# Retention and mixture-of-depths on one core: a new order for the routed work, and constant products on TensorE

## Chip, cores and metric

The kernel runs on 1 core of one Trainium2 chip. The metric is the device time of one execution in microseconds (us); lower is better.

## The reference

Inputs q, k, v have shape (4 batches, 8 heads, 768 tokens, 64). Step one is retention, a recurrence with a decay per head; step two picks 128 of the 768 tokens of each batch by a score and sends only those through a feed-forward block (512 to 1024 to 512).

```python
state = gamma[None, :, None, None] * state + np.einsum('bhd,bhe->bhde', k[:, :, t], v[:, :, t])
y[:, :, t] = scale * np.einsum('bhd,bhde->bhe', q[:, :, t], state)
...
x = np.ascontiguousarray(attn_out.transpose(0, 2, 1, 3)).reshape(B, S, H * D)
...
scores = np.einsum('bsd,d->bs', x, w_gate)
...
top_idx = np.argpartition(-scores[b], capacity)[:capacity]
h = np.maximum(xe @ w1, 0.0)
ye = h @ w2
g = 1.0 / (1.0 + np.exp(-scores[b, top_idx]))
out[b, top_idx] = x[b, top_idx] + g[:, None] * ye
```

## The kernel before

The 4 x 768 tokens are walked in 12 blocks of 256 tokens, three blocks to a batch; block m belongs to batch m // 3, and each block has two chunks of 128 tokens (u = 0, 1). The schedule is written out by hand: one turn of the main loop (L538) for each block, and every engine takes its instructions in the order in which the program issues them.

**A turn m, in program order.** SyncE (SP) issues the load of block m+4 (L540; for the last blocks at L561). POOL scales and casts block m+2 to bf16 (`cast`, L180: qb, kc, vb). TensorE (PE) transposes q of block m+1 (`transposes`, L192), multiplies the second half of the heads' scores (`scores(m, 1)`, L212, whose result VectorE (DVE) multiplies by the mask into am, L224), updates the state (`update`, L251), transposes k of block m+1, forms the output of block m (`inside`, L230, and `across`, L242). ScalarE (ACT) copies the output to xo and DVE multiplies it by w_gate and sums it into the token's score (`finish`, L267). SP writes xo to HBM (`put`, L289). PE then does `scores(m+1, 0)` and `turn_back(m+1)` (L202).

**The routed work** of a batch is cut into functions, and `at(t, place, f, ...)` (L479) hangs each on a place in a turn; `slot_work(t, place)` (L526) issues what hangs there. Places -1, 0, 1, 2, 3 to 5 stand in turn m ahead of the cast, after `update(m, 0)`, after the k transposes, after `put`, and at the turn's end. Within one place the functions come in the order in which L482 to L524 register them. After the last turn, what is left is issued in sorted order (L570), as turns 12 and 13. For the batch that ends in block m the steps are: rows, spread and beats (compare scores), ranks and pick (turn m+1, place 4), split, index and gate (turns m+1 and m+2), `route_fetch` (L414, POOL gathers the 128 rows from HBM by an indirect DMA), `route_turn` (L423, PE transposes them), `ffn_up` in two parts (L438), `ffn_down` (L454), `ffn_add` (L464, DVE), `route_put` (L470, POOL scatters the rows to HBM by an indirect DMA). Batches 0 and 1 fetch at place -1 of turns 6 and 9 and put at place 5 of turns 8 and 11. Batch 2 fetches in turn 10 and puts in turn 13, batch 3 does all of it in turns 12 and 13.

An indirect DMA names a range of HBM rows (`flat[:(b + 1) * S]`), so the fetch of batch b waits until earlier writes to these rows have landed, those of the puts of earlier batches too, and POOL's queue waits with it.

**PSUM.** Eight banks: pt (the transposes, one bank), pa (scores, two), py0 and py1 (outputs, one each), pst (state, one) and two slots of the tag pm, shared by pb, pr, rk, pi, pg, ph and pd. For batches 2 and 3 both parts of `ffn_up` write one two-bank tile in pa's place (L445), and batch 2's `ffn_down` writes in pt's place (L457). `inside` takes py0 and py1 itself (L232).

The lines to follow are

```python
    p, b, m = B - 2, B - 1, NBLK
    at(m - 1, 4, ffn_up, p, 0)
    at(m, 0, ffn_up, p, 1)
    at(m, 1, ffn_down, p)
    at(m + 1, 0, route_index, b)
    at(m + 1, 0, ffn_add, p)
    at(m + 1, 0, route_turn, b)
```

Of the kernel before, what the change touches and what calls it, by code (L numbers as in the profile page):

```python
# [9 lines left out]
FT = mybir.dt.float32  # L10
BF = mybir.dt.bfloat16
# [7 lines left out]
def kernel(ctx: ExitStack, tc: tile.TileContext, q, k, v, w_gate, w1, w2, capacity, out):  # L19
    nc = tc.nc  # L20
    B, H, S, D = q.shape
    C = 128
    NC = S // C
    T = 2 * C
    NM = S // T
# [49 lines left out]
    wgB = consts.tile([128, Dm], FT)  # L75
    nc.sync.dma_start(wgB, bass.AP(tensor=w_gate.tensor, offset=w_gate.offset, ap=[[0, 128], [1, Dm]]))

    part_i = consts.tile([128, 3], I32)  # L80
# [47 lines left out]
        nc.gpsimd.affine_select(out=causal[rows], in_=causal[rows], pattern=[[-1, 2], [1, C]],  # L128
                                compare_op=OP.is_ge, fill=0.0, base=0, channel_multiplier=-2)

    ones = consts.tile([128, 128], BF)
    nc.vector.memset(ones, 1.0)

    S_sb = [consts.tile([128, HP, 128], BF, name=f"S{j}") for j in range(2)]

# [10 lines left out]
    def route_tables():  # L146
        nc.gpsimd.memset(before, TINY)
        nc.gpsimd.affine_select(out=before, in_=before, pattern=[[1, C]], compare_op=OP.is_gt,
                                fill=-TINY, base=0, channel_multiplier=-1)
        slot_i = consts.tile([128, C], I32)  # L150
        nc.gpsimd.iota(slot_i, pattern=[[1, C]], base=0, channel_multiplier=0)
        nc.gpsimd.tensor_copy(slotrow, slot_i)
        tok_i = consts.tile([128, 2, NC], I32)
        nc.gpsimd.iota(tok_i[:, 0, :], pattern=[[0, NC]], base=0, channel_multiplier=1)
        nc.gpsimd.iota(tok_i[:, 1, :], pattern=[[C, NC]], base=0, channel_multiplier=0)
        nc.gpsimd.tensor_copy(tokc, tok_i.rearrange("p a c -> p c a"))
# [35 lines left out]
    def transposes(m, nm):  # L192
        src = nat[m][2 if nm == "q" else 0]
        pt = psT.tile([128, 8, T // 8, HP], BF, name="pt", tag="pt")
        for i in range(8):
            nc.tensor.transpose(pt[:, i].rearrange("p s g -> p (s g)"), src[:, i], ident)  # L196
        t = work.tile([128, HP, T], BF, name=nm + "T", tag=nm + "T")
        nc.scalar.activation(t.rearrange("p g (s i) -> p g s i", i=8), pt.rearrange("p i s g -> p g s i"), AF.Copy)  # L198
        tr[nm, m] = t
# [27 lines left out]

    def inside(m):  # L230
        vb = nat[m][1]
        py = [psY.tile([C, H, D], FT, name=f"py{u}", tag=f"py{u}") for u in range(2)]  # L232
        for h in range(H):
            dd, half = divmod(h, 2)
            for j in range(2):
                for u in range(2):
                    r = slice(u * 64, u * 64 + 64)
                    nc.tensor.matmul(py[u][:, h, :], att[m, dd // 2][r, half, dd % 2, j, :], vb[r, j, h, :],  # L238
                                     start=(h == 0 and j == 0), stop=True, skip_group_check=True)
        return py  # L240

    def across(m, u, py):  # L242
        i = 2 * m + u
# [169 lines left out]

    def route_fetch(b):  # L414
        st = batch[b]
        xg = perb.tile([128, Dm], FT, name="xg", tag="xg")
        rows, src, n = (st["idx"], flat[:(b + 1) * S], (b + 1) * S) if b < B - 1 else (st["own"], xs, S)
        nc.gpsimd.indirect_dma_start(
            out=xg, out_offset=None, in_=src, in_offset=bass.IndirectOffsetOnAxis(ap=rows[:, 0:1], axis=0),
            bounds_check=n - 1, oob_is_err=True)  # L420
        st["xg"] = xg
# [16 lines left out]
    def ffn_up(b, part):  # L438
        st = batch[b]
        n = FB // 2  # L440
        if b < B - 2:
            ph = psM.tile([128, n, C], FT, name="ph", tag="pm")
        else:
            if part == 0:
                st["ph"] = psA.tile([128, 2, n, C], FT, name="ph", tag="pa")  # L445
            ph = st["ph"][:, part]
        for j in range(n):
            ff = part * n + j
            for dd in range(DD):
                nc.tensor.matmul(ph[:, j, :], w1s[:, dd, ff * 128:(ff + 1) * 128], st["xT"][:, dd, :],  # L450
                                 start=(j == 0 and dd == 0), stop=True, skip_group_check=True)
        nc.scalar.activation(st["hT"][:, part * n:(part + 1) * n, :], ph, AF.Relu)

    def ffn_down(b):  # L454
        st = batch[b]
        if b == B - 2:
            pd = psT.tile([128, Dm], FT, name="pd", tag="pt")  # L457
        else:
            pd = psM.tile([128, Dm], FT, name="pd", tag="pm")
        for ff in range(FB):  # L460
            nc.tensor.matmul(pd, st["hT"][:, ff, :], w2s[:, ff, :], start=(ff == 0), stop=(ff == FB - 1))
        st["pd"] = pd

    def ffn_add(b):  # L464
        st = batch[b]
# [13 lines left out]
    def at(t, place, f, *args):  # L479
        slots.setdefault((t, place), []).append((f, args))  # L480

    for m in reversed(range(NBLK)):  # L482
        b, r = divmod(m, NM)
        at(m, 4, route_rows, b, r)
        at(m + 1, 0, route_spread, b, r)
        at(m + 1, 1, route_beats, b, r)
        if r == NM - 1:
            at(m + 1, 4, route_ranks, b)
            at(m + 1, 4, route_pick, b)
            if b < B - 1:  # L490
                at(m + 1, 5, route_split, b)
                at(m + 2, 0, route_index, b)
                at(m + 2, 4, route_gate, b)
                at(m + 3, 1, route_sigmoid, b)
            if b < B - 2:

                d = m + 4
                at(d, -1, route_fetch, b)
                at(d + 1, 0, route_turn, b)
                at(d + 1, 2, ffn_up, b, 0)  # L500
                at(d + 1, 4, ffn_up, b, 1)
                at(d + 2, 1, ffn_down, b)
                at(d + 2, 4, ffn_add, b)
                at(d + 2, 5, route_put, b)

    p, b, m = B - 2, B - 1, NBLK
    at(m - 2, 1, route_fetch, p)
# [1 line left out]
    at(m - 1, 4, ffn_up, p, 0)  # L509
    at(m - 1, 5, route_split, b)  # L510
    at(m, 0, ffn_up, p, 1)
    at(m, 1, ffn_down, p)
    at(m + 1, 0, route_index, b)
    at(m + 1, 0, route_fetch, b)
    at(m + 1, 0, ffn_add, p)
# [3 lines left out]
    at(m + 1, 1, ffn_up, b, 0)  # L519
    at(m + 1, 1, ffn_up, b, 1)  # L520
    at(m + 1, 2, route_sigmoid, b)
    at(m + 1, 2, ffn_down, b)
    at(m + 1, 3, ffn_add, b)
    at(m + 1, 3, route_put, b)  # L524

# [4 lines left out]
    cast(0)  # L530
    cast(1)
    route_tables()
    transposes(0, "q")
    transposes(0, "k")
    scores(0, 0)
    turn_back(0)

    for m in range(NBLK):  # L538
        if m < 6:
            load(m + 4)  # L540
        slot_work(m, -1)
        if m + 2 < NBLK:
            cast(m + 2)
        if m in (1, 3, 4, 6):
            load_weights((1, 3, 4, 6).index(m))
        if m + 1 < NBLK:
            transposes(m + 1, "q")
        scores(m, 1)
        update(m, 0)
        slot_work(m, 0)  # L550
        if m + 1 < NBLK:
            transposes(m + 1, "k")
        slot_work(m, 1)
        py = inside(m)
        for u in range(2):
            across(m, u, py)
        xo = finish(m, py)
        update(m, 1)
        put(m, xo)
        if m == 5:  # L560
            load(10)  # L561
            load(11)
        slot_work(m, 2)
        if m + 1 < NBLK:
            scores(m + 1, 0)
            turn_back(m + 1)
        slot_work(m, 3)
        slot_work(m, 4)
        slot_work(m, 5)
# [37 lines left out]
```

## Time and profile before

| | us |
|---|---|
| median of 3 runs | 125.67 |
| lowest, highest | 125.01, 129.92 |
| the profiled execution | 124.89 |
| its span, first to last instruction | 123.2 |

| engine | busy us | share of the span |
|---|---|---|
| PE | 85.1 | 69% |
| PE weight loads | 69.6 | 56% |
| DVE | 74.3 | 60% |
| ACT | 72.2 | 59% |
| POOL | 80.0 | 65% |

The times of the profile count from the span's start. No engine is busy for three quarters of the span, so the shares don't name a bound; it has to be looked for stretch by stretch, in what each engine waits for. The granted clock of PE is given as a share of full speed, 1.0 for 2.4 GHz and 0.5 for 1.2 GHz.

### The profile page before, as it was taken

What the parts mean: (1) busy time and instruction counts of PE and PEld (TensorE: products, weight loads), DVE (VectorE), ACT (ScalarE), POOL (GpSimd) and SP (SyncE); (2) the same over time, 40 slices, a digit from 0 to 9 for tenths busy, and PEclk for the clock granted to TensorE, in tenths of its full rate; (3) what the DMA queues carried; (4) which work ended last, traced back from release to release, by engine and by line L of the source; (5) the groups of instructions that cost most, each with busy time, mean ns of one, the idle gap of its engine ahead of it and who ended that gap; (6) DMA issues with size and microseconds to landing.
All of it is one profiled execution on the core that took longest, in us unless ns stands there. A gap on an engine that the chain in (4) does not pass through costs nothing. (4 is left out here: it accounts for less than half of the span.)

```text
span 123.2 us, 4327 instructions
## 1 busy us (share of the span) xinstructions
PE 85.1 (69%) x1808; PEld 69.6 (56%) x1812; DVE 74.3 (60%) x207; ACT 72.2 (59%) x115; POOL 80.0 (65%) x96
## 2 busy tenths in 40 slices
PE   0036798968678758767699689657489796777730
PEld 0024677756567647656588656546388564637500
DVE  6000348896999696699824773999072876825020
ACT  7133578896969578696756592956166854212300
POOL 6648999999958995874799737134995202425130
PEclk9999999999999995899855999965556999999997
DMA  2898999999999999999999999975800931721402
GB/s 57 294 272 306 358 340 365 339 341 379 262 348 369 354 279 330 322 288 350 386 359 347 277 327 357 374 268 192 254 3 8 287 144 49 291 85 21 154 0 85
DMA packets 26115, 31.47 MB, mean 256 GB/s; under 512 B 1648, under 2 KB 14960, under 8 KB 26096
## 3 DMA queue, kind: packets, MB, share of 16 engines
q1 hardware_dynamic: 23856, 27.01, 65.9%
q0 software_dynamic: 2240, 4.20, 14.9%
q8 instruction: 14, 0.23, 0.8%
q14 instruction: 5, 0.04, 0.1%
HBM read 24.38 MB, written 8.91 MB: 270 GB/s over the span
## 5 line engine op out<-in xcount | busy, mean ns | idle before, releaser
L224 DVE TENSOR_TENSOR am<-pa,causal 128x1024 bf16<-128x1024 f32 x24 | 29.3, 1221 | 19.0 <-PE pa L221 19.0
L185 POOL TENSOR_TENSOR qb<-qf,gq 128x1024 bf16<-128x1024 f32 x12 | 22.8, 1903 | 5.3 <-DMA qf<-in_q_dram 5.2
L188 POOL TENSOR_TENSOR vb<-vf,gv 128x1024 bf16<-128x1024 f32 x12 | 22.8, 1903 | 3.1 <-DMA vf<-in_v_dram 3.1
L277 DVE SCALAR_TENSOR_TENSOR junk<-py,wgB 128x512 bf16<-128x512 f32 x24 | 15.6, 688 | 14.3 <-PE py L248 14.2
L274 ACT ACTIVATE xo<-py 128x512 f32<-128x512 f32 x24 | 14.3, 597 | 14.1 <-PE py L248 6.2
L198 ACT ACTIVATE qT<-pt 128x1024 bf16<-128x1024 bf16 x12 | 12.3, 1029 | 8.4 <-PE pt L196 8.4
L221 PE MATMUL pa<-qT,kT 64*64 64x128 bf16 x384 | 11.9, 240 | 7.2 <-DVE am L224 6.1
L196 PE MATMUL pt<-ident,qb 128*128 128x128 bf16 x96 | 8.6, 242 | 11.0 <-POOL qb L185 11.0
L187 POOL CAST kc<-kf 128x1024 bf16<-128x1024 f32 x12 | 12.4, 1037 | 5.0 <-DMA kf<-in_k_dram 5.0
L198 ACT ACTIVATE kT<-pt 128x1024 bf16<-128x1024 bf16 x12 | 12.3, 1023 | 4.4 <-PE pt L196 4.4
L221 PEld LDWEIGHTS <-kT 64*64 64x64 bf16 x384 | 8.3, 116 | 9.3 <-issue 6.4
L209 ACT ACTIVATE kb<-pb 128x1024 bf16<-128x1024 bf16 x12 | 12.3, 1026 | 2.1 <-PE pb L207 2.0
L196 PEld LDWEIGHTS <-qb 128*128 128x128 bf16 x96 | 6.6, 108 | 11.5 <-POOL qb L185 11.4
L450 PE MATMUL ph<-xT,w1s 128*128 128x128 bf16 x128 | 9.1, 229 | 4.9 <-ACT xT L434 2.1
L238 PE MATMUL py<-vb,am 64*128 64x64 bf16 x384 | 10.2, 208 | 3.2 <-DVE am L224 2.6
L265 ACT ACTIVATE S<-pst 128x512 bf16<-128x512 f32 x20 | 12.0, 600 | 0.5
L196 PE MATMUL pt<-ident,kc 128*128 128x128 bf16 x96 | 9.6, 257 | 2.9 <-POOL kc L187 1.5
L450 PEld LDWEIGHTS <-w1s 128*128 128x128 bf16 x128 | 8.3, 103 | 5.7 <-issue 5.6
L238 PEld LDWEIGHTS <-am 64*128 64x128 bf16 x384 | 8.1, 106 | 5.9 <-DVE am L224 3.0
L263 PE MATMUL pst<-vb,kb 64*64 64x64 bf16 x320 | 10.0, 206 | 1.1 <-issue 1.1
L472 POOL DMA_INDIRECT out_dram<-ye,idx x4 | 4.2, 1046 | 9.9 <-DVE ye L467 4.8
L196 PEld LDWEIGHTS <-kc 128*128 128x128 bf16 x96 | 8.2, 117 | 4.1 <-issue 1.9
(88 smaller groups left out, 146.4 us busy)
## 6 DMA issues: line engine op xcount, KB each, us to landing
qf<-in_q_dram SPq DMA_DIRECT2D x24, 256.0 KB, 7.0
kf<-in_k_dram SPq DMA_DIRECT2D x24, 256.0 KB, 7.5
vf<-in_v_dram SPq DMA_DIRECT2D x12, 512.0 KB, 8.8
out_dram<-xo SPq DMA_DIRECT2D x24, 256.0 KB, 6.3
xs<-xo SPq DMA_DIRECT2D x6, 256.0 KB, 2.9
w1s<-in_moe_w_dram POOLq DMA_DIRECT2D x2, 512.0 KB, 8.9
w2s<-in_moe_w_dram POOLq DMA_DIRECT2D x2, 512.0 KB, 11.1
wgB<-in_moe_w_gate_dram SPq DMA_DIRECT2D x1, 256.0 KB, 7.2
```

Of the source, the lines that this page charges most:

```text
L185: nc.gpsimd.tensor_mul(qb, raw["q", m].rearrange("p h j d -> p j h d"), gq[:, r, :, :, None].to_broadcast([128, 8, 2, D]))
L187: nc.gpsimd.tensor_copy(kc, raw["k", m].rearrange("p h j d -> p j h d"))
L188: nc.gpsimd.tensor_mul(vb, raw["v", m].rearrange("p h j d -> p j h d"), gv[:, 2 * r:2 * r + 2, :, None].to_broadcast([128, 2, H, D]))
L196: nc.tensor.transpose(pt[:, i].rearrange("p s g -> p (s g)"), src[:, i], ident)
L198: nc.scalar.activation(t.rearrange("p g (s i) -> p g s i", i=8), pt.rearrange("p i s g -> p g s i"), AF.Copy)
L209: nc.scalar.activation(kb.rearrange("p j h d -> p (j h d)"), pb.rearrange("p j g x -> p (j g x)"), AF.Copy)
L221: nc.tensor.matmul(pa[u * 64:u * 64 + 64, half, d, j, :], kT[r, dd, u * C:(u + 1) * C].rearrange("p (s j) -> p s j", j=2)[:, :, j], qT[r, ...
L224: nc.vector.tensor_mul(am.rearrange("p a b c d -> p (a b) (c d)"), pa.rearrange("p a b c d -> p (a b) (c d)"), causal.rearrange("p a b -> ...
L238: nc.tensor.matmul(py[u][:, h, :], att[m, dd // 2][r, half, dd % 2, j, :], vb[r, j, h, :], start=(h == 0 and j == 0), stop=True, skip_grou ...
L274: nc.scalar.activation(xo[:, u, :], py[u].opt(), AF.Copy)
L277: nc.vector.scalar_tensor_tensor(junk, py[w].opt(), 1.0, wgB, OP.mult, OP.mult, accum_out=batch[b]["sc"][:, 2 * r + w:2 * r + w + 1])
L450: nc.tensor.matmul(ph[:, j, :], w1s[:, dd, ff * 128:(ff + 1) * 128], st["xT"][:, dd, :], start=(j == 0 and dd == 0), stop=True, skip_group ...
```

## The change

Five things are done.

- `ones` is set at the start, and `fill(py, n)` issues n matmuls of `ones` with a 512-column moving operand of ones into the output banks, whose results `inside` overwrites. 12 stand ahead of the first transposes, 2 after each of the first two, and 2 (in turns 1, 2, 4, 5) or 4 (turns 3, 6, 9) between `transposes(m + 1, "q")` and `scores(m, 1)`. py0 and py1 are taken there, ahead of `inside`.
- The fetches of batches 0 and 1 move from place -1 of turns 6 and 9 to place 5 of turns 5 and 8. The put of batch 0 moves from place 5 of turn 8 to place 5 of turn 9. xg gets three buffers.
- `ffn_down` is issued in halves, the first from the first four blocks of hT. Batch 1's first half moves to place -1 of turn 11; batch 2's second half moves behind `route_ranks` and `route_pick` of batch 3 (place 5 of turn 12).
- For batches 2 and 3 the first part of `ffn_up` writes in pa's place and the second in pt's.
- Batch 2's `ffn_down` now writes to a slot of pm.

```diff
+    ones = consts.tile([128, 128], BF)
+    nc.vector.memset(ones, 1.0)
...
+    def output_banks():
+        return [psY.tile([C, H, D], FT, name=f"py{u}", tag=f"py{u}") for u in range(2)]
+
+    def fill(py, n):
+        for i in range(n):
+            nc.tensor.matmul(py[i % 2], ones, ones[:, None, :].to_broadcast([128, 4, 128]),
+                             start=True, stop=True, skip_group_check=True)
...
-        xg = perb.tile([128, Dm], FT, name="xg", tag="xg")
+        xg = perb.tile([128, Dm], FT, name="xg", tag="xg", bufs=3)
...
-        if b < B - 2:
-            ph = psM.tile([128, n, C], FT, name="ph", tag="pm")
-        else:
-            if part == 0:
-                st["ph"] = psA.tile([128, 2, n, C], FT, name="ph", tag="pa")
-            ph = st["ph"][:, part]
+        pool, tag = (psM, "pm") if b < B - 2 else ((psA, "pa"), (psT, "pt"))[part]
+        ph = pool.tile([128, n, C], FT, name="ph", tag=tag)
...
+    def ffn_down(b, part):
+        st = batch[b]
+        if part == 0:
+            st["pd"] = psM.tile([128, Dm], FT, name="pd", tag="pm")
+        n = FB // 2
+        for ff in range(part * n, (part + 1) * n):
+            nc.tensor.matmul(st["pd"], st["hT"][:, ff, :], w2s[:, ff, :], start=(ff == 0), stop=(ff == FB - 1))
...
-                d = m + 4
-                at(d, -1, route_fetch, b)
...
-                at(d + 2, 1, ffn_down, b)
-                at(d + 2, 4, ffn_add, b)
-                at(d + 2, 5, route_put, b)
+                d = m + 3
+                at(d, 5, route_fetch, b)
...
+                at(d + 3, -1 if b else 1, ffn_down, b, 0)
+                at(d + 3, 1, ffn_down, b, 1)
+                at(d + 3, 4, ffn_add, b)
+                at(d + (3 if b else 4), 5, route_put, b)
...
-    at(m, 1, ffn_down, p)
+    at(m, 1, ffn_down, p, 0)
+    at(m, 5, ffn_down, p, 1)
...
+    py = output_banks()
+    fill(py, 12)
     transposes(0, "q")
+    fill(py, 2)
     transposes(0, "k")
+    fill(py, 2)
...
+        if m:
+            py = output_banks()
+
+        if 1 <= m < 7 or m == 9:
+            fill(py, 4 if m % NM == 0 else 2)
         scores(m, 1)
```

## Rows read from the trace of the kernel before

**Rows 1.** The page: PE's granted clock in 40 slices of 3.08 us.

```profile
PEclk9999999999999995899855999965556999999997
```

**Rows 2.** Timeline of the head, POOL then PE: start, length, [idle <- releaser].

```profile
57.00 1.89 POOL L185 TENSOR_TENSOR qb<-qf,gq 128x1024 bf16<-128x1024 f32 x1 [2.15 <-DMA qf<-in_q_dram]
...
58.95 0.62 PE L196 MATMUL pt<-ident,qb 128*128 128x128 bf16 x8 [1.22 <-POOL qb L185]
...
73.91 1.02 PE L461 MATMUL pd<-w2s,hT 128*128 128x512 bf16 x4 [0.26 <-DMA w2s<-in_moe_w_dram]
```

**Rows 3.** Timeline of PE, turns 9 and 10.

```profile
78.60 0.42 PE L221 MATMUL pa<-qT,kT 64*64 64x128 bf16 x16 [1.19 <-DVE am L224]
...
81.72 0.61 PE L238 MATMUL py<-vb,am 64*128 64x64 bf16 x16 [1.31 <-DVE am L224]
...
87.86 1.03 PE L196 MATMUL pt<-ident,qb 128*128 128x128 bf16 x8 [2.47 <-POOL qb L185]
...
90.96 1.11 PE L432 MATMUL pg<-identf,xg 128*128 128x128 f32 x4 [0.32 <-DVE idx L392]
...
94.70 0.44 PE L263 MATMUL pst<-vb,kb 64*64 64x64 bf16 x16
```

**Rows 4.** Timeline of POOL, from turn 8's cast to batch 1's fetch.

```profile
75.67 1.90 POOL L188 TENSOR_TENSOR vb<-vf,gv 128x1024 bf16<-128x1024 f32 x1 [0.91 <-DMA vf<-in_v_dram]
80.82 1.11 POOL L472 DMA_INDIRECT out_dram<-ye,idx  x1 [3.25 <-DMA out_dram<-xo]
84.81 1.06 POOL L418 DMA_INDIRECT xg<-out_dram,idx  x1 [2.88 <-DMA out_dram<-ye,idx]
```

**Rows 5.** DMA issues from 66.1 to 80 us: times, KB, us to landing.

```profile
out_dram<-xo SPq DMA_DIRECT2D x6, 256.0 KB, 6.4
qf<-in_q_dram SPq DMA_DIRECT2D x2, 256.0 KB, 9.0
```

**Rows 6.** The first put's landing, then the timeline of SP's queue.

```profile
out_dram<-ye,idx POOLq DMA_INDIRECT x1, 3.7
...
51.57 3.70 SPq L295 DMA_DIRECT2D out_dram<-xo  x2
...
66.17 3.80 SPq L64 DMA_DIRECT2D qf<-in_q_dram  x2
...
72.00 5.96 SPq L295 DMA_DIRECT2D out_dram<-xo  x6
```

**Rows 7.** Timeline of POOL, the first fetch.

```profile
53.70 1.15 POOL L418 DMA_INDIRECT xg<-out_dram,idx  x1 [0.16 <-DMA out_dram<-xo]
```

**Rows 8.** Timeline of DVE, end of turn 9 and turn 10.

```profile
85.44 0.96 DVE L366 TENSOR_TENSOR pick<-rk,slotrow 128x768 bf16<-128x768 f32 x1
89.52 1.22 DVE L224 TENSOR_TENSOR am<-pa,causal 128x1024 bf16<-128x1024 f32 x1 [3.12 <-PE pa L221]
```

**Rows 9.** Timeline of PE: `ffn_up` at half clock, then the tail.

```profile
65.78 1.74 PE L450 MATMUL ph<-xT,w1s 128*128 128x128 bf16 x16
...
106.66 1.05 PE L450 MATMUL ph<-xT,w1s 128*128 128x128 bf16 x16 [0.47 <-ACT hT L452]
107.76 1.67 PE L461 MATMUL pd<-w2s,hT 128*128 128x512 bf16 x7
109.27 0.67 PE L357 MATMUL rk<-ones,beats 128*128 128x1 bf16 x21
...
111.19 1.50 PE L429 MATMUL pg<-pick,xb 128*128 128x128 bf16 x24
...
115.23 1.05 PE L450 MATMUL ph<-xT,w1s 128*128 128x128 bf16 x16 [0.74 <-ACT hT L452]
```

**Rows 10.** Timeline of DVE, the tail.

```profile
111.51 0.21 DVE L392 TENSOR_SCALAR idx<-pi 128x1 int32<-128x1 f32 x1
111.64 0.74 DVE L467 SCALAR_TENSOR_TENSOR ye<-pd,gt,xg 128x512 f32<-128x512 f32 x1
```

**Rows 11.** Window of the tail: length; PE, PEld, DVE, ACT, POOL busy; clock; DMA.

```profile
104.92:123.20 18.28, 10.11 (x138) 7.44 (x139) 5.77 (x19) 3.08 (x6) 5.27 (x10) 0.96 0.29 102
```

More of the change, by code (lines that the diff above doesn't have):

```diff
@@ L129 @@
                                 compare_op=OP.is_ge, fill=0.0, base=0, channel_multiplier=-2)
-    ones = consts.tile([128, 128], BF)
-    nc.vector.memset(ones, 1.0)
     S_sb = [consts.tile([128, HP, 128], BF, name=f"S{j}") for j in range(2)]
@@ L226, in scores, with inside @@
         att[m, part] = am
-    def inside(m):
+    def inside(m, py):
         vb = nat[m][1]
-        py = [psY.tile([C, H, D], FT, name=f"py{u}", tag=f"py{u}") for u in range(2)]
         for h in range(H):
@@ L239, in inside @@
                                      start=(h == 0 and j == 0), stop=True, skip_group_check=True)
-        return py
     def across(m, u, py):
@@ L452, in ffn_up @@
         nc.scalar.activation(st["hT"][:, part * n:(part + 1) * n, :], ph, AF.Relu)
-    def ffn_down(b):
+    def ffn_down(b, part):
         st = batch[b]
[L456 to L462, printed above, removed]
+        if part == 0:
[3 more added lines that the diff above has]
+            nc.tensor.matmul(st["pd"], st["hT"][:, ff, :], w2s[:, ff, :], start=(ff == 0), stop=(ff == FB - 1))
     def ffn_add(b):
@@ L495 @@
             if b < B - 2:
-                d = m + 4
-                at(d, -1, route_fetch, b)
-                at(d + 1, 0, route_turn, b)
-                at(d + 1, 2, ffn_up, b, 0)
-                at(d + 1, 4, ffn_up, b, 1)
-                at(d + 2, 1, ffn_down, b)
-                at(d + 2, 4, ffn_add, b)
-                at(d + 2, 5, route_put, b)
+                d = m + 3
+                at(d, 5, route_fetch, b)
+                at(d + 2, 0, route_turn, b)
+                at(d + 2, 2, ffn_up, b, 0)
+                at(d + 2, 4, ffn_up, b, 1)
+                at(d + 3, -1 if b else 1, ffn_down, b, 0)
+                at(d + 3, 1, ffn_down, b, 1)
+                at(d + 3, 4, ffn_add, b)
+                at(d + (3 if b else 4), 5, route_put, b)
     p, b, m = B - 2, B - 1, NBLK
@@ L521 @@
     at(m + 1, 2, route_sigmoid, b)
-    at(m + 1, 2, ffn_down, b)
+    at(m + 1, 2, ffn_down, b, 0)
+    at(m + 1, 2, ffn_down, b, 1)
     at(m + 1, 3, ffn_add, b)
@@ L553 @@
         slot_work(m, 1)
-        py = inside(m)
+        inside(m, py)
         for u in range(2):
```

## The prediction

> **What bounds the kernel now.** I read the windows and slices first, then each engine's waits in order of time, and looked for the place up to which the loads set the pace. On PE the turn that begins at 58.95 waits for qb of block 8, and POOL, which makes it, had waited 2.15 us for the load of q [rows 2]. At 73.91 PE waits again for a transfer, the second half of w2, inside batch 0's `ffn_down` [rows 2]. So up to about 74 us the kernel goes as fast as its transfers, and an edit that only shortens PE's, ACT's or DVE's work there is given back in one of these two waits. From there on it is a chain on the chip, and two things stretch it.
>
> The first is POOL's queue. It is free at 77.57 (75.67 + 1.90), issues batch 0's put at 80.82, when ye is there, then stands until the put has landed, and gathers for batch 1 at 84.81 [rows 4]. Only behind that, at 85.9, may block 11 be cast, though its q load, issued from 66.17 to 69.97 and 9.0 us under way, had landed by 79.0 [rows 5, 6]. PE waits 2.47 us for that cast [rows 3], and DVE, which masks the scores that come next, has 3.12 us of idle time [rows 8].
>
> The second is PE's clock. It is at half (1.2 GHz) in the slices from 80 to 95 us and at full (2.4 GHz) on both sides [rows 1]. PE's idle times ahead of the fall are only 1.19 and 1.31 us [rows 3].
>
> Then comes a tail of 18.28 us from batch 2's first part of `ffn_up` to the end [rows 11], in which PE, ACT and DVE hand work to each other and little overlaps.
>
> **The change, part by part.** All sums are against the profiled execution, 124.89 us.
>
> *Fills ahead of 74 us.* By batch 2's `ffn_down`, whose eight matmuls of 512 columns take 1.51 us (107.76 to 109.27) [rows 9], one costs 0.19 us at full clock, and 0.31 at half by the ratio below. The 16 at the start stand where PE has nothing to do but wait for the first loads, and those of turns 1 to 6 (2 or 4 each) stand in waits for DVE like that of 1.19 us [rows 3]. If a few tenths of them stick out, the 1.22 us wait at 58.95 takes them [rows 2]. I take 0. Below nothing isn't possible while the loads decide; the upper bound, with all 16 fills of turns 1 to 6 at half clock and uncovered, is 5.0 - 1.2 = 3.8 us.
>
> *The first fetch.* On POOL's queue place 5 of turn 5 and place -1 of turn 6 are the same place, between the casts of blocks 7 and 8. Nothing changes: 0.
>
> *Batch 1's fetch and batch 0's put.* The fetch now goes at 77.6, ahead of the put, takes 1.1 us of POOL, and block 11's cast follows at about 79.0, when its load is in: qb at 80.9. PE has issued its ranks by 85.39 (87.86 - 2.47), so the wait for qb goes altogether. What is late next is DVE: the mask product that began at 89.52 can't pass pick, which ends at 86.40 (85.44 + 0.96) [rows 8]. PE has time to be ready by then if the clock is full (85.39 + 0.62 for the transposes + 0.42 for the scores = 86.43). So this piece is worth 3.1 us at full clock, and 2.5 us (PE's wait) at half. The put goes behind block 11's cast and the small casts of turn 9, at some 87; the next fetch, batch 2's in turn 10, then waits for its landing, 3.7 us [rows 6], so that it goes at about 91 and lands another 4 later. PE transposes its rows only in turn 11, after 95, so the moved wait costs 0; if the landing took 3 us more it would begin to cost, at most those 3.
>
> *The fills of turn 9.* Four in PE's wait of 1.19 us (78.60) [rows 3]: 0.76 us, hidden. Their use is the clock. The ratio between the levels is read from one shape: 16 matmuls of `ffn_up` took 1.74 us at half and 1.05 at full [rows 9], 0.60. If the clock stays full, the dense stretch of turn 10 from 90.96 to 94.70 (3.74 us) [rows 3] shrinks by 0.40 x 3.74 = 1.5 us; half-clock work ahead of that is already in the 3.1. I take 1.5: turn 9's idle sum falls from 2.5 to 1.7 us and the 2.47 us hole behind it is gone. The other end, 0, is a rival below.
>
> The Trainium skill (TensorE: Matmul & The Clock Gate, section Why this matters for your kernels) warns only of idle gaps longer than any in rows 3. By that rule the clock would not have fallen at 80, the fills would buy nothing, and the sum would be the same, since the new order alone would keep it full. The trace doesn't agree: it fell after gaps of 1.19 and 1.31 us, so a second fall stays possible.
>
> *Batch 1's `ffn_down` in halves.* The whole stood ahead of `inside(11)` and still does, so PE's sum is the same. Four matmuls (0.76 us) now precede `scores(11, 1)`, and DVE's mask product is that much later, beside the second half. I take 0, bounds 0 and 0.76.
>
> *The tail.* Batch 2's second part of `ffn_up` waited 0.47 us for ACT's hT of the first part (106.66), batch 3's 0.74 us (115.23) [rows 9]; with banks of their own both waits go. Moving four of batch 2's eight `ffn_down` matmuls behind the ranks brings these 0.76 us forward, and the four lie beside DVE's pick (0.96 us for the same operation [rows 8]). Together 0.47 + 0.76 = 1.2 us up to the ranks, and 0.74 later. One part costs: pd of batch 2 now sits in a slot of pm until ye has read it, and pi has the other, so batch 3's `route_turn`, which began at 111.19 [rows 9], must wait for one of them: for idx, 111.72, or for ye, 112.38 [rows 10]. That is 0.5 or 1.2 us. I take 0.5, because the same step of batch 1 (90.96) began right behind idx [rows 3], that is in pi's slot.
>
> *Added instructions* (36 matmuls with their weight loads) are issue time in waits; 0.
>
> Sum: 3.1 + 1.5 + 1.2 - 0.5 + 0.7 = 6.0, so 118.9 us. The median of the runs shown, 125.67, lies 0.8 above the profiled execution and the lowest 0.1 above; I add 0.4: **119.3 us**. Own range 117.3 to 121: the pm slot (+0.7), the half `ffn_down` (+0.8), the place of the run within the spread, and 1.5 us below if the earlier put and the denser PE shorten ACT's and DVE's waits too.
>
> **The rivals.**
>
> *The clock falls again.* The 1.31 us wait for DVE at 81.72 stays, and in turn 10 PE must still wait for pick and idx. Then 2.5 + 0 + 1.2 - 0.5 + 0.7 = 3.9: 121.0, with the 0.4 121.4. For it: the fall after such short gaps. Against: 0.76 us more work in just that turn and no hole behind it.
>
> *The fetch still holds POOL.* It reads rows of batches 0 and 1; if it had to wait for SP's writes of later blocks, six of which are issued from 72.00 to 77.96 and land 6.4 us after [rows 5, 6], it would go at 84.4 and block 11's cast would be where it was. Then only the tail gains: 1.4, so 123.5, with the 0.4 123.9: no change that can be told. Against: batch 0's fetch was issued at 53.70 [rows 7], while SP was still issuing two writes from 51.57 to 55.27 [rows 6], so it doesn't wait for rows that it doesn't read.
>
> *Slower: the clock falls and doesn't come back.* It returned at about 95 us in a stretch of batch 1's `ffn_up`, after 7 us of dense half-clock PE work from 87.86 [rows 1, 3]. If the new order breaks that work up by waits (idx, kb) and the clock stays at half to the end, the tail's 10.11 us of PE [rows 11] become 16.8, +6.7, and batch 1's two parts of `ffn_up` and its `ffn_down` add 2 x 0.69 + 1.0 = 2.4. With the 3.9 of the first rival: 124.9 - 3.9 + 9.1 = 130.1, with the 0.4 130.5. It decides as soon as about two thirds of that work runs at half (+6.4 against 3.9 is 127.8). Against: the tail has shorter waits than before, and before it ran at 0.96.
>
> **How the numbers follow.** Forecast 0.60, the clock's second fall 0.24, the held fetch 0.10, the slower tail 0.06. A measurement of this kernel can tell about 2% from no change, so the bounds are 123.16 and 128.18. Faster: 0.60 and nearly all of the 0.24, 0.82. Same: the held fetch and 0.02 of the second rival's spread, 0.12. Slower: 0.06. The range for 8 in 10 takes the forecast and the clock's second fall with their spreads, and on its upper side part of the uncovered fills: 116.0 to 123.0.
>
> **What would show it.** Right: POOL issues the fetch within 0.3 us of block 10's cast and block 11's cast follows; PE's 2.47 us wait for qb is gone and DVE's mask product comes right behind pick; the slices from 80 to 95 are at full clock; `ffn_up`'s second parts of batches 2 and 3 start without a wait for hT; batch 3's turn starts right behind idx. The turns up to 74 us keep their length. Wrong: half clock after 80 (the first rival), a fetch that starts after 84 (the second), or a head that is longer because fills stick out between transposes and scores. The forecast fails altogether if the stretch before 74 us isn't set by transfers.

## The result, and the profile after

The changed kernel takes 119.11 us (median of 4 runs, 118.81 to 119.35), the kernel before, beside it on the same chip, 125.84 (4 runs). The ratio is 0.9485 with a 95% interval of 0.9427 to 0.9543. The profiled execution took 119.3 us, its span is 117.6. Forecast were 119.3 for the median and 118.9 for the profiled execution. Ratios and their intervals compare only executions within 1.5% of the fastest of their kernel, medians take in all of them, and the profiles of e4, e5 and e10 below are of slower executions.

The two traces can be cut at the same events. The starts are taken from timelines of PE.

| stretch | before, us | after, us | difference | forecast |
|---|---|---|---|---|
| start to the transposes of block 10's q (turn 9) | 76.80 | 76.08 | -0.72 | 0 |
| from there to those of block 11's q (turn 10) | 11.06 | 7.20 | -3.86 | -3.1 |
| from there to batch 2's first part of `ffn_up` | 17.06 | 17.23 | +0.17 | -1.5 |
| the tail | 18.28 | 17.09 | -1.19 | -1.4 |
| sum | 123.20 | 117.60 | -5.60 | -6.0 |

The sum came out within 0.4 us, in part by luck. The stretch of the order gave 0.76 us more than forecast, and the start 0.72 us that belong to no term and are less than two executions of one kernel differ by. Together they stand in for the 1.5 us of the clock, of which nothing is left in the third row.

The timeline of POOL after, from block 10's last cast to batch 2's fetch. It answers to [rows 4].

```profile
74.93 1.90 POOL L199 TENSOR_TENSOR vb<-vf,gv 128x1024 bf16<-128x1024 f32 x1 [0.85 <-DMA vf<-in_v_dram]
76.99 1.11 POOL L427 DMA_INDIRECT xg<-out_dram,idx  x1 [0.16 <-DMA kf<-in_k_dram]
78.13 1.92 POOL L196 TENSOR_TENSOR qb<-qf,gq 128x1024 bf16<-128x1024 f32 x1
...
85.91 1.08 POOL L475 DMA_INDIRECT out_dram<-ye,idx  x1 [0.71 <-DMA out_dram<-xo]
90.93 1.06 POOL L427 DMA_INDIRECT xg<-out_dram,idx  x1 [3.94 <-DVE junk L286]
```

The fetch goes 0.16 us behind block 10's cast and block 11's qb right behind it, 3.2 us behind block 10's vb, where before it came 10.2 behind it. The put has moved to 85.91, and the wait for its landing now stands ahead of batch 2's fetch, 3.94 us, where nothing is queued that PE needs soon. (The releaser named there is the event that came last by the profile, DVE's junk, long done by then; in e7 below the same wait, 2.98 us, is put down to the put.)

The timeline of PE after, turns 9 and 10 [rows 3]:

```profile
76.75 1.04 PE L88 MATMUL py<-ones 128*128 128x512 bf16 x4
77.88 0.42 PE L232 MATMUL pa<-qT,kT 64*64 64x128 bf16 x16
...
81.00 0.41 PE L248 MATMUL py<-vb,am 64*128 64x64 bf16 x16 [1.31 <-DVE am L235]
...
83.28 0.61 PE L207 MATMUL pt<-ident,qb 128*128 128x128 bf16 x8
84.41 0.42 PE L232 MATMUL pa<-qT,kT 64*64 64x128 bf16 x16 [0.53 <-DVE am L235]
...
86.54 0.66 PE L441 MATMUL pg<-identf,xg 128*128 128x128 f32 x4 [0.91 <-DVE idx L401]
...
89.70 0.63 PE L272 MATMUL pst<-vb,kb 64*64 64x64 bf16 x16
```

The 2.47 us wait for qb is gone. The four constant products fill the former wait of 1.19 us, and the scores follow without one. In turn 10 a short wait for am has appeared (0.53), and the one for idx has grown (0.91, before 0.32).

DVE after, where PE now has to wait for it [rows 8], and the page's row of the granted clock in 40 slices of 2.94 us [rows 1]:

```profile
84.28 0.95 DVE L375 TENSOR_TENSOR pick<-rk,slotrow 128x768 bf16<-128x768 f32 x1
85.14 1.21 DVE L235 TENSOR_TENSOR am<-pa,causal 128x1024 bf16<-128x1024 f32 x1
```

```profile
PEclk9999967999999999999975699999985999999995
```

The mask product stands right behind pick. The distance from the start of pick to the start of am is 0.86 us, before it was 4.08: 3.22 less, forecast 3.1. And the clock fell all the same, only later and for a shorter time: before it was at half from about 81 to 94.5 us, now from about 87.3 to 90.7. The windows of the two middle stretches and of three pieces around that fall (length; PE, PEld, DVE, ACT, POOL busy; granted clock; DMA share; GB/s):

```profile
76.08:83.28 7.20, 5.74 (x156) 4.42 (x153) 7.17 (x20) 5.28 (x8) 7.02 (x6) 1.00 0.89 317
83.28:100.51 17.23, 13.31 (x270) 10.52 (x267) 11.75 (x30) 11.16 (x19) 6.03 (x13) 0.90 0.46 163
86.50:88.00 1.50, 1.46 (x22) 1.26 (x24) 0.77 (x4) 0.73 (x2) 0.49 (x1) 0.77 0.36 128
88.00:89.50 1.50, 1.50 (x38) 1.41 (x32) 0.00 (x0) 1.02 (x2) 0.00 (x0) 0.50 0.20 68
89.50:91.00 1.50, 1.50 (x29) 1.24 (x27) 1.20 (x3) 0.94 (x2) 0.07 (x1) 0.60 0.13 46
```

In turn 9 DVE is busy for 7.17 of 7.20 us: it, and no longer POOL, sets that turn. The half clock lies on just the dense stretch of turn 10 (`inside`, `across`, `update`) that the clock term spoke of.

The tail after, PE and then DVE [rows 9, 10]:

```profile
101.62 1.06 PE L455 MATMUL ph<-xT,w1s 128*128 128x128 bf16 x16
102.52 1.03 PE L465 MATMUL pd<-w2s,hT 128*128 128x512 bf16 x4
103.38 0.67 PE L366 MATMUL rk<-ones,beats 128*128 128x1 bf16 x21
...
103.93 1.02 PE L465 MATMUL pd<-w2s,hT 128*128 128x512 bf16 x4
...
105.89 1.51 PE L438 MATMUL pg<-pick,xb 128*128 128x128 bf16 x24 [0.45 <-DVE idx L401]
107.24 0.29 PE L408 MATMUL pg<-parts,pick 128*128 128x3 bf16 x6
108.75 1.95 PE L455 MATMUL ph<-xT,w1s 128*128 128x128 bf16 x32 [1.22 <-ACT xT L443]
```

```profile
105.61 0.21 DVE L401 TENSOR_SCALAR idx<-pi 128x1 int32<-128x1 f32 x1
105.75 0.74 DVE L470 SCALAR_TENSOR_TENSOR ye<-pd,gt,xg 128x512 f32<-128x512 f32 x1
```

Both second parts of `ffn_up` start without a wait for hT (batch 3's two parts are one run of 32), and the ranks stand between the halves of `ffn_down`. Batch 3's turn waits 0.45 us and starts behind idx, ahead of ye's end: the slot of pm costs what was forecast.

### The profile page after: what moved, and what is told of

The parts are those of the page before. It is cut to its first block, busy times and chain, and to the rows that moved or that the text cites. A ratio compares the mean times of both kernels' runs of the same rounds, so it can differ in the third digit from the quotient of the medians.

```text
span 117.6 us, 4402 instructions
## 1 busy us (share of the span) xinstructions
PE 89.3 (76%) x1848; PEld 67.1 (57%) x1848; DVE 74.0 (63%) x207; ACT 71.8 (61%) x115; POOL 79.9 (68%) x96
## 5 line engine op out<-in xcount | busy, mean ns | idle before, releaser
L232 PE MATMUL pa<-qT,kT 64*64 64x128 bf16 x384 | 11.3, 225 | 2.3 <-DVE am L235 1.0
L88 PE MATMUL py<-ones 128*128 128x512 bf16 x36 | 11.5, 449 | 1.2 <-DVE ones L79 1.1
L207 PE MATMUL pt<-ident,qb 128*128 128x128 bf16 x96 | 7.4, 220 | 6.0 <-POOL qb L196 6.0
L232 PEld LDWEIGHTS <-kT 64*64 64x64 bf16 x384 | 7.6, 108 | 7.3 <-issue 4.7
L248 PE MATMUL py<-vb,am 64*128 64x64 bf16 x384 | 9.4, 203 | 1.9 <-DVE am L235 1.9
L207 PEld LDWEIGHTS <-qb 128*128 128x128 bf16 x96 | 5.5, 98 | 8.5 <-POOL qb L196 8.4
L248 PEld LDWEIGHTS <-am 64*128 64x128 bf16 x384 | 7.6, 103 | 4.4 <-DVE am L235 2.1
L207 PE MATMUL pt<-ident,kc 128*128 128x128 bf16 x96 | 8.1, 231 | 2.5 <-POOL kc L198 1.5
```

The lines of the kernel that those rows point to most:

```text
L232: nc.tensor.matmul(pa[u * 64:u * 64 + 64, half, d, j, :], kT[r, dd, u * C:(u + 1) * C].rearrange("p (s j) -> p s j", j=2)[:, :, j], qT[r, ...
```

## The experiments

They ran in three groups, each on one chip with the kernel before beside it (medians there 126.06, 125.20 and 127.09 us, 11 runs each). The start of turn 9 moves from execution to execution (76.08, 76.99 and 81.04 us in the three profiles of the changed kernel alone; up to 82 us POOL waited 12.5 us for loads in the first and 15.2 us in the last), so next to the ratio stand the stretches cut as above. A dash stands where the comparison gave no interval.

| kernel | ratio [95%] | median, us | turn 9 | to `ffn_up` (clock) | tail |
|---|---|---|---|---|---|
| before | | | 11.06 | 17.06 (0.80) | 18.28 |
| changed | 0.9485 [0.9427, 0.9543] | 119.11 | 7.20 | 17.23 (0.90) | 17.09 |
| e0, changed again | 0.9514 [0.9425, 0.9603] | 119.35 | 7.20 | 17.09 (0.90) | 16.52 |
| e10, changed, third | 0.9429 [0.9338, 0.9519] | 119.96 | 7.32 | 17.59 (0.90) | 17.15 |
| e1, old order | - | 125.66 | 12.04 | 17.47 (0.78) | 17.15 |
| e7, order alone | 0.9783 [0.9702, 0.9864] | 121.80 | 7.21 | 17.09 (0.81) | 18.27 |
| e3, old tail | 0.9700 [0.9654, 0.9747] | 122.31 | 7.20 | 17.75 (0.90) | 18.92 |
| e11, tail alone | 0.9852 [0.9771, 0.9934] | 124.21 | 10.88 | 17.81 (0.76) | 17.09 |
| e4, pd in the state's bank | - | 120.38 | 7.21 | 15.64 (1.00) | 16.40 |
| e2, no fills | - | 121.53 | 7.20 | 16.24 (1.00) | 17.04 |
| e9, no fills again | 0.9563 [0.9460, 0.9665] | 120.70 | 7.20 | 16.27 (1.00) | 17.13 |
| e5, fills of turn 9 alone | 0.9512 [0.9397, 0.9628] | 119.74 | 7.20 | 16.90 (0.90) | 16.48 |
| e6, more fills | 0.9495 [0.9428, 0.9563] | 118.21 | 7.20 | 15.65 (1.00) | 16.43 |
| e8, more fills and that bank | 0.9420 [0.9366, 0.9474] | 118.52 | 7.20 | 16.30 (1.00) | 16.35 |

Groups: e1 to e4; e0, e5, e6, e7; e8 to e11. Where an expectation names theories by letters, it says what they are.

### The order: e1 and e7

e1 is the changed kernel with the fetches of batches 0 and 1 and the put of batch 0 where they were.

```diff
-                at(d, 5, route_fetch, b)
+                at(d + 1, -1, route_fetch, b)
...
-                at(d + (3 if b else 4), 5, route_put, b)
+                at(d + 3, 5, route_put, b)
```

> The changed kernel with batch 0's put back at place 5 of turn 8 and the fetches back at place -1 of turns 6 and 9; fills, halves and banks stay. Theory (the order carries about 60% of the gain): POOL again stands from about 77 us until ye and until the put has landed, block 11's cast begins after 84, PE waits over 2 us for qb in turn 10 and its clock is at half behind that wait. 2.5 us for the wait plus up to 1.3 us of half clock: about 122.8 us, 122 to 123.5. Rival (the fills and the clock carry the gain, the order is worth little): about 119 to 120 us.

Measured: 125.66 us (4 runs, 124.08 to 126.72), beside a median before of 126.06. That is 2.2 us above the upper end of what was expected: in the time nearly everything that the change gained is gone. The timeline of POOL of e1, then that of PE:

```profile
80.87 1.11 POOL L475 DMA_INDIRECT out_dram<-ye,idx  x1 [3.33 <-DMA out_dram<-xo]
85.82 1.06 POOL L427 DMA_INDIRECT xg<-out_dram,idx  x1 [3.84 <-DMA out_dram<-ye,idx]
86.90 1.92 POOL L196 TENSOR_TENSOR qb<-qf,gq 128x1024 bf16<-128x1024 f32 x1
```

```profile
81.77 0.41 PE L248 MATMUL py<-vb,am 64*128 64x64 bf16 x16 [1.31 <-DVE am L235]
88.88 1.03 PE L207 MATMUL pt<-ident,qb 128*128 128x128 bf16 x8 [4.69 <-POOL qb L196]
```

The fetch waits for the put and qb for the fetch, as in [rows 4]. That it costs 4.84 us here (12.04 against 7.20) and not 3.86 comes from the put: POOL stood 3.84 us for its landing, before it stood 2.88. The fills of turn 9 are in this kernel too, and its PE, at full clock up to the wait, was through with the turn sooner than before; only the wait for qb grew, from 2.47 to 4.69. A faster PE in front of this wait gained nothing. Nor does the time say that the order is the whole gain: the tail keeps its own here (17.15 against 18.28), and what hides it is the later landing (about 1 us) and a longer turn 10 (17.47 against 17.06 up to the tail, both with half clock in them).

e7 is the opposite: the kernel before with the new order and the third buffer of xg, nothing else.

```diff
-        xg = perb.tile([128, Dm], FT, name="xg", tag="xg")
+        xg = perb.tile([128, Dm], FT, name="xg", tag="xg", bufs=3)
...
-                d = m + 4
-                at(d, -1, route_fetch, b)
...
+                d = m + 3
+                at(d, 5, route_fetch, b)
...
-                at(d + 2, 5, route_put, b)
...
+                at(d + (3 if b else 4), 5, route_put, b)
```

> The kernel before with only the new order of the fetches of batches 0 and 1 and of the put of batch 0, and three buffers for xg: no fills, ffn_down whole, banks and tail as before. Theory (the order carries most of the gain; undoing it cost all): block 11's cast begins at about 79, PE's wait for qb in turn 10 is gone, and 4.0 to 5.0 us are won: 121 to 122 us. Rival (the order pays only together with the fills, since the clock falls without them): 2.5 us won, 123.3 us. Batch 3's xT shows whether its later start comes with the order: 0.1 us behind the last product if not.

Measured: ratio 0.9783 (0.9702 to 0.9864), 121.80 us, 3.4 under the median before of its group where 4 to 5 were expected. The windows of e7, the same three stretches:

```profile
77.43:84.64 7.21, 4.71 (x151) 4.12 (x149) 7.18 (x20) 5.29 (x8) 7.02 (x6) 0.98 0.83 296
84.64:101.73 17.09, 14.35 (x270) 11.60 (x269) 11.84 (x30) 11.35 (x19) 6.11 (x13) 0.81 0.46 162
101.73:120.00 18.27, 10.11 (x138) 7.45 (x139) 5.77 (x19) 3.08 (x6) 5.27 (x10) 0.96 0.29 102
```

Turn 9 has its 7.21 us without a single constant product, and the other two stretches are those of before (17.06 and 18.28) within 0.03. So no fill is needed for the 3.85 us of turn 9. A part of them hangs on the clock, though. In this profile turn 9 is at full clock and the fall comes in turn 10; in the kernel before the clock fell inside turn 9 (0.50 from 81.00 us), and pick began 8.64 us after the turn's transposes. In every other profile it began 8.19 to 8.32 us after them, in e1 (8.20) and e11 (8.19) too, which have the old order and a full clock up to there. So 0.44 us hang on the full clock of turn 9, which neither the order nor the fills decide, and about 3.4 would be left without it (an estimate from these starts of pick). With full clock on both sides the order is worth 10.88 - 7.20 = 3.68 us by e11 and 4.84 by e1, where the put landed later.

### The tail: e3, e11 and e4

e3 is the changed kernel with the old tail: both parts of `ffn_up` of batches 2 and 3 in one two-bank tile in pa's place, batch 2's pd in pt's place and its `ffn_down` whole ahead of the ranks.

```diff
...
-    at(m, 5, ffn_down, p, 1)
+    at(m, 1, ffn_down, p, 1)
```

> The changed kernel with the tail as it was: both parts of ffn_up of batches 2 and 3 in one two-bank tile, batch 2's ffn_down whole ahead of the ranks and in the bank of the transposes. Theory: the ranks come 1.2 to 1.5 us later and the last ffn_up waits 0.74 us for hT again, but batch 3's turn no longer waits for idx (0.5): 1.4 to 1.8 us lost, about 120.7 us. Rival (the tail's end is set by the last gather or by the put of batch 2): 119.1 us.

Measured: ratio 0.9700 (0.9654 to 0.9747), tail 18.92 us. The timeline of PE of e3:

```profile
102.92 1.05 PE L459 MATMUL ph<-xT,w1s 128*128 128x128 bf16 x16 [0.46 <-ACT hT L461]
...
105.77 0.67 PE L366 MATMUL rk<-ones,beats 128*128 128x1 bf16 x21
...
112.20 1.05 PE L459 MATMUL ph<-xT,w1s 128*128 128x128 bf16 x16 [0.74 <-ACT hT L461]
```

Both waits for hT are back at their old sizes, and the ranks stand 4.59 us behind the start of `ffn_up` (105.77 - 101.18, the start of the tail) where the changed kernel has 2.87. The tail's part of the change is 18.92 - 17.09 = 1.83 us by this pair, as was expected (1.4 to 1.8). The whole time lost more, 2.15% by the ratios: 0.52 us of it lie ahead of the tail (17.75 against 17.23), where the edit changes nothing. They go with the clock's fall, which differs from profile to profile, and with the late releases of the last section.

e11 puts that tail alone into the kernel before: the new banks, pd in a slot of pm, batch 2's second half of `ffn_down` behind the ranks.

```diff
...
-    at(m, 1, ffn_down, p)
+    at(m, 1, ffn_down, p, 0)
+    at(m, 5, ffn_down, p, 1)
...
```

> The kernel before with the change's tail alone: batch 2's ffn_down in halves around the ranks, the parts of ffn_up in banks of their own, pd in a slot of pm; old order, no fills. If the terms add up: the stretch from batch 2's ffn_up to the end falls from 18.28 us to 16.5 to 17.1, all else as before, so 1.2 to 1.8 us under the kernel before, about 124.0. Rival (the tail's gain shows only where the stretch ahead is shorter, since batch 2's rows and the ranks then come earlier): the waits for hT go but the end moves by less than 0.7 us, 124.8 or more.

Measured: ratio 0.9852 (0.9771 to 0.9934), tail 17.09 us against 18.28. The windows of e11:

```profile
76.72:87.60 10.88, 4.84 (x151) 4.15 (x149) 9.11 (x21) 6.65 (x9) 4.96 (x5) 0.92 0.82 287
87.60:105.41 17.81, 15.00 (x263) 12.26 (x265) 10.02 (x28) 10.24 (x17) 8.21 (x14) 0.76 0.29 99
105.41:122.50 17.09, 9.99 (x138) 7.44 (x139) 5.77 (x19) 3.19 (x6) 5.30 (x10) 0.93 0.31 110
```

The tail's gain is there without the new order, so the rival of this run falls. e7 and e11 together (2.2% and 1.5%) leave some 1.5% of the 5.15% for all else. Each of the three numbers has an interval of 0.6 to 0.8% to either side, and the changed kernel's ratio itself is 0.9429 to 0.9514 over its three groups: what the remainder is, or that it is more than nothing, isn't settled by them.

e4 is the changed kernel with batch 2's pd in the state's bank, whose last use is over by then, so that both slots of pm are free for pi and pg.

```diff
-            st["pd"] = psM.tile([128, Dm], FT, name="pd", tag="pm")
+            pool, tag = (psS, "pst") if b == B - 2 else (psM, "pm")
+            st["pd"] = pool.tile([128, Dm], FT, name="pd", tag=tag)
```

> The changed kernel with batch 2's ffn_down result in the bank of the state, which nothing needs any more, instead of in a slot of pm. Theory (the slot costs what idx makes batch 3's turn wait): the turn starts right behind the index products, 0.5 us earlier, 118.6 us. In the changed kernel's trace xT of batch 3 started another 0.6 us behind the last product that it reads; if that also comes from the slot, the gain is 1.1 us, 118.0 us. Rival (the turn waits for something else at the same time): 119.1 us.

Measured: 120.38 us (6 runs, 117.14 to 123.63), no ratio; the time is inconclusive, the trace is not. The timeline of PE of e4:

```profile
106.32 0.30 PE L395 MATMUL pi<-tokc,pick 128*128 128x2 bf16 x6 [0.18 <-DVE pick L375]
106.48 1.50 PE L438 MATMUL pg<-pick,xb 128*128 128x128 bf16 x24
```

The turn starts 0.16 us behind the index products, in the changed kernel 0.76 (105.89 - 105.13): the slot costs 0.6 us, and its holder is the one that the forecast named. The tail is shorter by 0.69 us (16.40 against 17.09), and in the pair e8 and e10 by 0.80.

### The constant products: e2, e5, e6, e8, e9, with e0 and e10

e2 is the changed kernel without any fill, e5 has the four of turn 9 alone.

```diff
-        for i in range(n):
+        for i in range(0):
```

> The changed kernel with no fill issued at all, so without the products of ones; all else stays. Theory (fills matter only where they hold the clock in turn 9): the clock is at half again from about 80 us into turn 10, instead of from 87 to 91; DVE covers part, so 0.7 to 1.5 us are lost: about 120.2 us. Rival A (idle gaps as short as these don't cost the clock, so the fills buy nothing): 119.1 us, with the clock at full after 80. Rival B (the fills at the start warm PE and shorten the turns ahead of 74 us, and that is where the gain is): the turn of block 9 begins later than 77.5 and the time is over 121.5 us.

```diff
-    fill(py, 12)
...
-    fill(py, 2)
...
-    fill(py, 2)
...
-        if 1 <= m < 7 or m == 9:
+        if m == 9:
```

> The changed kernel with only the four fills of turn 9; those at the start and in turns 1 to 6 are gone. Without any fill the median was 121.5 us, 2.4 above the changed kernel. Theory A (only the fills of turn 9 matter, they hold the clock beside the chain that sets the end): the time of the unaltered kernel of this group, within 0.5 us. Theory B (the early fills matter, by a steadier clock ahead of 74 us): 1.5 to 2.5 us above it, with the turn of block 9 beginning later. Theory C (the fills buy nothing, the 121.5 was the chip): all of this group alike, and this one as the one without fills.

> The changed kernel unaltered, on the same chip as the three other runs of this group, to compare them with it: about 119.1 us if this chip is like the first, its ratio to the kernel before 0.945 to 0.96 in any case.

Measured: e2 121.53 us (118.47 to 122.47) in the first group; e5 0.9512 beside e0 at 0.9514 in the second. The fills ahead of turn 9 buy nothing that can be measured. e2's trace goes against the theory of its run and with rival A: the clock is at full from turn 9 into the tail, and turn 9 begins at 76.82, so rival B's sign isn't there either. But its median looked like a loss of 2.4 us against the changed kernel's, which ran elsewhere, so it was run once more beside it:

> The changed kernel without any constant products, beside the unaltered changed kernel on one chip. If the change's fills buy something: slower than it by 1.5 to 2.2 us, as the medians of the first group (121.5) and of the unaltered kernel elsewhere (119.1 to 119.4) suggest. If they buy nothing: within 0.5 us of it, and the 121.5 came from the chip and the loads' arrival. In either case the stretch from the transposes of turn 9 to those of turn 10 is 7.2 us, since the order sets it.

> The changed kernel unaltered, for comparison with the three beside it: 119.3 (118.8 to 120). From the transposes of turn 9: block 11's transposes at +7.20, batch 2's ffn_up at +23 to +24.5 by the clock in turn 10, the end at +40 to +41.5.

Measured: e9 0.9563 (0.9460 to 0.9665), e10 0.9429 (0.9338 to 0.9519). The point is 1.3% worse without fills, and the intervals overlap. The traces don't show where it would come from: from the transposes of turn 9 to the end e9 takes 40.60 us, e10 42.06. That is past the 41.5 expected of e10, whose clock fell and whose ACT and DVE were released late (last section). The page's clock row of e9, and its timeline of PE:

```profile
PEclk9999999999995557999555799999999999999999
```

```profile
78.40 0.42 PE L232 MATMUL pa<-qT,kT 64*64 64x128 bf16 x16 [1.19 <-DVE am L235]
...
81.53 0.41 PE L248 MATMUL py<-vb,am 64*128 64x64 bf16 x16 [1.31 <-DVE am L235]
...
84.94 0.42 PE L232 MATMUL pa<-qT,kT 64*64 64x128 bf16 x16 [0.53 <-DVE am L235]
...
87.06 0.66 PE L441 MATMUL pg<-identf,xg 128*128 128x128 f32 x4 [0.91 <-DVE idx L401]
```

Here are all four waits, the 1.19 us that the fills close among them, and the granted clock is 1.00 from the transposes of turn 9 to the end. In the changed kernel three of the four are left and it falls. So neither the waits nor the fills of turn 9 decide alone whether the clock falls in turn 10. In six profiles of kernels whose PE work is the same from turn 7 to there, it fell in five (the changed kernel, e0, e10, e3, e5, the 0.90 of the table) and in one (e4) it did not. Of three kernels without fills whose PE work is the same there it fell in one (e7, 0.81) and in two (e2, e9) it did not. What decides it stays open.

e6 adds fills in turn 10's own waits, and four in turn 7.

```diff
+    def hold(n):
+        fill(now[0], n)
+
+    now = [None]
...
+                if b:
+                    at(m + 2, 0, hold, 3)
...
-        if 1 <= m < 7 or m == 9:
+        now[0] = py
+        if 1 <= m < 8 or 9 <= m < 11:
```

> The changed kernel with fills in turns 7 and 10 too, which have none: two behind the q transposes and three between batch 1's (batch 0's) index products and the next turn's transposes, where PE waited 0.5 and 0.9 us. Theory (the clock's fall at 87 us still costs): full clock in turn 10, 0.40 x 3.2 = 1.2 us less than the unaltered kernel of this group, and in turn 7 nothing or little, because the second half of w2 lands only at about 73 us. Rival (ACT's copies and DVE set turn 10's length, so that PE's clock there is covered): no difference.

e8 is e6 with e4's bank.

> The changed kernel with the added fills of turns 7 and 10 and with batch 2's pd in the state's bank. Theory A (work in turn 10's own waits holds the clock there): the granted clock stays full from about 80 us to the end, batch 2's ffn_up starts 22.9 us after the transposes of turn 9, batch 3's route_turn right behind its index products, 27.6 us after the same point, the end 38.8 after it; against the unaltered changed kernel beside it about 1.5 us for the clock and 0.5 for the bank, 117.3. Theory C (where the clock falls is chance, the added fills buy nothing): some slices of turn 10 are at half again, batch 2's ffn_up starts 24.3 after the transposes of turn 9, and only the bank's 0.5 us shows, 118.8.

Measured: e6 0.9495 beside e0 at 0.9514, e8 0.9420 beside e10 at 0.9429. By the ratios neither differs from the changed kernel. In e8 too the clock is full up to the tail, as its theory A has it, but batch 2's `ffn_up` starts 23.50 us after the transposes of turn 9 instead of 22.9, and the end comes at 39.85 instead of 38.8; the last section says why. The windows of e6:

```profile
77.02:84.22 7.20, 5.74 (x155) 4.42 (x153) 7.17 (x21) 5.27 (x8) 7.01 (x6) 1.00 0.81 290
84.22:99.87 15.65, 12.99 (x275) 9.61 (x273) 11.76 (x30) 10.98 (x19) 5.99 (x13) 1.00 0.52 177
99.87:116.30 16.43, 9.99 (x138) 7.44 (x139) 5.76 (x19) 3.08 (x6) 5.28 (x10) 1.00 0.32 114
```

The clock is full over all three. The second stretch takes 15.65 us, in e0, on the same chip and with the clock at 0.90, 17.09: the fall in turn 10 costs 1.44 us in this pair. Up to batch 1's first part of `ffn_up` the stretch takes 5.78 to 5.80 us in all five profiles of the new order at full clock, and 6.93 to 7.26 in the six in which the clock fell, so a fall costs 1.1 to 1.5 us there. That size is shown. That the added fills prevent it is not: e6 and e8 show no fall in one profile each, but nor do e2, e9 and e4, without them. The medians of e6 and e8, 118.21 and 118.52, are the lowest of the study, and their 12 runs lie between 117.76 and 119.66, the changed kernel's 17 between 117.80 and 124.77; with ratios that can't be told apart, neither is claimed to beat the changed kernel. The bank is the one part of e8 whose gain a trace shows: 0.6 us at the start of the turn.

## Why the prediction was right

*What bounds the kernel.* Nothing speaks against it: the change put 16 fills into turns 1 to 6 and 16 ahead of the first turn, and the transposes of turn 9 start at 76.08 against 76.80, a difference smaller than that between two executions of one kernel (e0 76.99, e10 81.04). No run shortened PE's or POOL's work there, so that the transfers alone set the pace is argued from the waits and not shown. Fills ahead of 74 us at nothing: right, e5 against e0.

*The order.* Right, with its place: fetch behind block 10's cast, qb behind the fetch, DVE's mask product behind pick. The step from pick to am shrank by 3.22 us (forecast 3.1 at full clock). The term came to 3.86 because pick itself comes 0.44 us earlier in the turn (8.20 after the transposes, before 8.64); the last 0.2 are only lent, since am begins 1.86 behind block 11's transposes, before 1.66. In the sum this piece was put at the moment from which DVE is late; that PE, at full clock in turn 9, also hands DVE its ranks sooner, was left out. That part hangs on the clock of that turn, which is full in e1 and e11 with the old order too. It did not take the fills: e7 has the same 7.21 us.

*The moved wait.* Right: the put went at 85.91 (forecast 87), POOL then stood 3.94 us (3.7), the fetch went at 90.93 (91), and PE first needs its rows behind 98. It cost nothing.

*The clock.* Here the step failed: "If the clock stays full, the dense stretch of turn 10 from 90.96 to 94.70 (3.74 us) shrinks by 0.40 x 3.74 = 1.5 us". The size holds: up to batch 1's first part of `ffn_up` turn 10 took 7.21 us before and 5.78 to 5.80 where the clock stayed full, 1.4 less. The condition doesn't: in the changed kernel the clock fell at 87.3 us, the dense stretch shrank only from 3.74 to 3.16 us, and of the 7.21 us 6.98 are left. Behind that, 0.20 us were lost to the end of the half clock (that `ffn_up` took 1.27 us, before 1.07) and 0.20 in the stretch after it, where DVE's mask product began 0.48 us late (last section): -0.23 + 0.40 = +0.17. The reason given for a full clock, less idle time in turn 9, is not the one that decides, as e9 shows. The first rival, then, described the clock rightly and the order wrongly: it priced the order at 2.5, at half clock, while turn 9 ran at full, and so came out at 121.4 us. That the forecast's 119.3 was met and not this is owed to the order's larger term and to the start.

The rule of the Trainium skill (TensorE: Matmul & The Clock Gate, section Why this matters for your kernels), that idle gaps longer than any in turns 9 and 10 of these two kernels bring the clock down, agrees with e9 and not with the changed kernel, whose clock fell behind waits of 1.31, 0.53 and 0.91 us. In the kernel before, the prediction has it fall after the wait of 1.31 us; it fell within it (0.90 from 80.40 to 81.00, 0.50 from 81.00 to 81.60, and PE's work went on at 81.72).

*The tail.* Forecast -1.4, measured -1.19 in the pair of the forecast, -1.83 by e3, -1.19 by e11. Up to the ranks it gained 1.48 us (4.35 to 2.87 from the start of `ffn_up`; forecast 1.2), the slot cost 0.6 (0.5), batch 3's wait for hT (0.74) is gone. What pulled the pair down to 1.19 is a late start of ACT that belongs to no part of the change (last section).

*The other rivals.* The held fetch didn't come: 76.99, not 84. The clock at half to the end didn't come in any run.

## What to carry to other kernels

Here an indirect read queued behind an indirect write of the same range made the issuing engine stand until the write had landed (2.88 us before, 3.84 in e1), and everything queued behind it stood too. In such a case put the read first, and the write where its landing is waited for by nobody. Price such a reorder at the engine that is late next (here DVE), and don't add a term for the clock on the strength of one profile: a fall was worth 1.1 to 1.5 us in turn 10, it came in some executions and not in others of like work, and the fall inside turn 9 that the forecast started from is in no other profile. Cut traces at the same events, not at the same times, when the loads' arrival moves the whole by more than the edit does.

## What the runs showed that was not expected

A release by PE that comes late. In the changed kernel's tail batch 3's xT began 0.70 us behind the modelled end of the turn's products (108.10 against 105.89 + 1.51), in the kernel before 0.10 (112.79 against 111.19 + 1.50), with the same instructions. The timeline of ACT, first the changed kernel, then e0, which is the same kernel:

```profile
108.10 0.60 ACT L443 ACTIVATE xT<-pg 128x512 bf16<-128x512 f32 x1 [4.79 <-PE pg L408]
```

```profile
108.27 0.60 ACT L443 ACTIVATE xT<-pg 128x512 bf16<-128x512 f32 x1 [4.18 <-PE pg L438]
```

The first names the gate products (L408) that are issued behind the turn, the second the turn itself (L438). The late form (0.57 to 0.75 us) is in the tails of the changed kernel and of all profiles of the first and the third group, the early one (0.10) in all of the second and in the kernel before. It accounts for the tail of one and the same kernel, 17.09, 16.52 and 17.15 us (changed, e0, e10), and for e7, in the second group, having the tail of before to 0.01. Compared within a form, the tail's gain is 18.28 - 16.52 = 1.76 us in the early one and 18.92 - 17.09 = 1.83 in the late one, against a forecast of 1.4. It comes neither with the slot of pm, since e4 and e8 have it, nor with the order, since e1 and e11 have it and e7 doesn't.

The same lateness stands in turn 10, and there it explains why that stretch has two lengths at full clock in the table, 15.64 and 15.65 us in e4 and e6, 16.24 to 16.30 in e2, e9 and e8. The copy kb<-pb on ACT reads the products pb. First e9, PE and ACT, then e6:

```profile
90.94 0.62 PE L218 MATMUL pb<-ident,kT 128*128 128x128 bf16 x8
...
92.01 1.02 ACT L220 ACTIVATE kb<-pb 128x1024 bf16<-128x1024 bf16 x1 [0.37 <-PE pg L408]
```

```profile
91.36 0.62 PE L218 MATMUL pb<-ident,kT 128*128 128x128 bf16 x8
...
92.02 1.02 ACT L220 ACTIVATE kb<-pb 128x1024 bf16<-128x1024 bf16 x1
```

In e9 kb begins 0.45 us behind the modelled end of pb, in e6 0.04. DVE's mask product of that turn begins 0.39 to 0.94 us behind the scores that it reads in e2, e3, e8, e9 and e10, 0.48 in the changed kernel, and 0.05 to 0.15 in all others. From batch 1's first part of `ffn_up` to batch 2's it takes 9.84 to 9.86 us in e0, e4, e5 and e6 and 10.25 to 10.66 in the changed kernel, e2, e3, e8, e9 and e10. Here e4 has the early form, and so have e1 and e11, so a group doesn't share one form throughout. What sets it stays open; no run settles it.

The landing of a put. POOL stood 2.88 us for batch 0's before, 3.84 in e1, with the same kernel code around it. Where this wait is on the path, as in e1, it moves the time by about 1 us on its own.
